# Score matmuls in 64x64 TensorE tiles without a block-diagonal K, K transposed in another order and copied by VectorE, and odd V rows moved by VectorE, in a fused sliding-window attention and adapter kernel

## The chip, the cores and the metric

One core of one Trainium2 chip. The metric is the device time of one execution in microseconds (us). A run is called fast or slow by the rule that these measurements use: for a program on one core, slow means over 1.5% above the fastest run of the same kernel. The profile is one execution taken by the hardware profiler; its span is 1.5 to 2.5 us shorter than the device time.

Names in the profile: PE is TensorE, PEld its weight loads, DVE is VectorE, ACT is ScalarE, POOL is GpSimd, SP issues the output DMAs. L312 is line 312 of the kernel that is being profiled, so the same statement has other line numbers in other kernels.

## The reference

```python
# 8 batches, 8 heads, 576 positions, head dimension 64; q, k, v are randn * 0.1, f32
scores = (q @ k.transpose) / sqrt(64)
scores = where(abs(i - j) <= 32, scores, -1e9)
attn   = softmax(scores) @ v                      # -> x, 4608 rows of 512
logits = x @ w_gate                               # 8 experts, the best 2 get softmax weights
out    = x + sum over the 2 experts of w * ((x @ A[e]) @ B[e])      # rank 16
```

## The kernel before

The work goes by head groups `y`: 16 of them, two per batch, four heads each, in two halves `t` of two heads `uu`. The stages of one group are: load Q, K, V with a cast to f16 (GpSimd issues these DMAs); transpose Q and K on TensorE; copy them out of PSUM (`f_q`, `f_k`); score matmuls (`f_score`); exp on ScalarE; PV matmuls; normalise on VectorE. Per batch the adapter stage follows. A list scheduler inside the program lays out a fixed order for every engine from assumed durations (the numbers in `plan.add`), and each engine then works through its own queue in order.

The parts that the change and the argument touch:

```python
kT  = [const.tile([128, 2 * NB, 2, 64], F16, ...)]     # partitions (t, d); columns (t, q, j): block-diagonal in t
vbd = [const.tile([128, NB, 4 * VC], F16, ...)]        # partitions (uu, t, 32 keys); V block-diagonal in (t, uu)

def f_k(y, t, eng):                # K out of PSUM: contiguous read, scattered write
    p0 = 64 * t
    tp = f16(("t", y, 1))[p0:p0 + 64, :, 0:576].rearrange("p v (j b q) -> p v j b q", j=8, b=18)
    dst = kT[y % NKT][p0:p0 + 64].rearrange("p b v (t q j) -> p t v j b q", t=2, q=4)[:, t]
    for jv in range(2):
        nc.scalar.copy(out=dst[:, jv], in_=tp[:, jv])          # 64 x 576, q steps by 8 elements = 16 bytes

def f_score(i):                    # 128x64 tiles: both halves t in one matmul, zeros between them
    ...
    nc.tensor.matmul(out=pt[64 * uu:64 * uu + 64, 4 * g:4 * g + 4],
                     lhsT=ident[:, 64 * uu:64 * uu + 64], rhs=bcast(mask, 1, 2), ...)
    nc.tensor.matmul(out=pt[64 * uu:64 * uu + 64, e]..., lhsT=kT[y % NKT][:, NB * uu + a, jv],
                     rhs=qT[y % NQT][:, :, c0:c0 + 8]..., ...)
...
    T["ek", y, t] = plan.add("ACT", 1.35, f_k(y, t, "ACT"), ...)    # the plan takes 1.35 us for two copies
```

The softmax here doesn't subtract the row's maximum and nothing guards it: scores larger than these inputs give would overflow.

Of the kernel before, what the change touches and what calls it, by code (L numbers as in the profile page):

```python
# [16 lines left out]
D_TR, D_S, D_PV, D_X, D_Z, D_G, D_O = -4.0, 0.0, 3.0, 4.0, 8.0, 4.0, 4.0  # L17
# [131 lines left out]
def kernel(  # L149
# [24 lines left out]
    VC = 2 * D + 2  # L174
    OC = D + 2
# [24 lines left out]
    kT = [const.tile([128, 2 * NB, 2, 64], F16, name=f"kT{i}") for i in range(NKT)]  # L200
    vbd = [const.tile([128, NB, 4 * VC], F16, name=f"vbd{i}") for i in range(NV)]
    PT = [const.tile([128, TB, 128], F16, name=f"PT{i}") for i in range(NPT)]
    xs = [const.tile([128, NG, DD], F16, name=f"xs{i}") for i in range(NX)]
    ident = const.tile([128, 128], F16)
    sel = const.tile([128, 4], F32)
    mask = const.tile([128, 2, 128], F16)
# [16 lines left out]
    def load_v(y):  # L223
        b, x = divmod(y, 2)
        d = vbd[y % NV]
        for uu in range(2):
            for t in range(2):
                c = 2 * t + uu
                s0 = 64 * uu + 32 * t
                src = v[b, 2 * x + uu + 4 * t].rearrange("(a p v) d -> p a (v d)", p=32, v=2)  # L230
                nc.gpsimd.dma_start(out=d[s0:s0 + 32, :, VC * c + 1:VC * c + 1 + 2 * D], in_=src)  # L231

    def zero_v(i):
        nc.vector.memset(vbd[i].rearrange("p a c -> p (a c)").bitcast(U32), 0)
        for z in (0, VC - 1):
            ones = vbd[i].rearrange("p a (c w) -> p a c w", c=4)[:, :, :, z]
            nc.vector.tensor_copy(out=ones, in_=bcast(sel, 1, NB))
# [4 lines left out]
    nc.vector.tensor_reduce(  # L242
        out=sel.rearrange("p (t u) -> p u t", t=2),
        in_=ident.rearrange("k (u t p) -> k u t p", u=2, t=2), axis=AX.X, op=ALU.add)
    zero_v(0)
# [3 lines left out]
    nc.vector.memset(kT[0].rearrange("p a b c -> p (a b c)").bitcast(U32), 0)  # L249
    nc.gpsimd.memset(mask, 0.0)  # L250
    for s in range(4):
        for jv in range(2):
            blk = mask[32 * s:32 * s + 32, jv].rearrange("k (u j p) -> k u j p", u=2, j=16)
            nc.gpsimd.affine_select(out=blk, in_=blk, compare_op=ALU.is_ge, fill=NEG,
                                    base=-jv, channel_multiplier=-2,
                                    pattern=[[64, 2], [1, 16], [16, 4]])
            nc.gpsimd.affine_select(out=blk, in_=blk, compare_op=ALU.is_ge, fill=NEG,
                                    base=64 + jv, channel_multiplier=2,
                                    pattern=[[-64, 2], [-1, 16], [-16, 4]])
# [3 lines left out]
    zero_v(1)  # L263
    load_v(1)
    for i in range(1, NKT):
        nc.vector.memset(kT[i].rearrange("p a b c -> p (a b c)").bitcast(U32), 0)
    for y in (2, 3):
        load(y, 0)
        load(y, 1)
        zero_v(y)  # L270
        load_v(y)
        if y == 2:
            for cc in range(4):
                nat = cc // 2 + 2 * (cc % 2)
                nc.gpsimd.dma_start(out=WA_sb[:, cc, 0:ER],
                                    in_=moe_A.transpose([1, 0, 2])[128 * nat:128 * nat + 128])
                nc.gpsimd.dma_start(out=WA_sb[:, cc, ER:],
                                    in_=moe_w_gate[128 * nat:128 * nat + 128])
            nc.gpsimd.dma_start(out=B_sb, in_=moe_B.rearrange("e r d -> (e r) d"))
# [3 lines left out]
    def f_tr(y, w):  # L283
        def fn():
            tp = f16(("t", y, w))
            src = raw[y, w]
            for s in range(NJ):
                j = s if w == 0 else 2 * (s % 8) + s // 8
                for t in range(2):
                    nc.tensor.matmul(out=tp[64 * t:64 * t + 64, s // 8, 72 * (s % 8):72 * (s % 8) + 72],  # L290
                                     lhsT=src[:, t, D * j:D * j + D],
                                     rhs=ident[0:72, 0:72], is_transpose=True,
                                     start=True, stop=True)
        return fn

    def f_q(y):
        def fn():
            tp = f16(("t", y, 0))[:, :, 0:576].rearrange("p h (j c) -> p h j c", j=8)
            dst = qT[y % NQT][:, :, 2:2 + 2 * NP].rearrange("p (h j) c -> p h j c", h=2)
            nc.vector.tensor_copy(out=dst, in_=tp)  # L300
        return fn

    def f_k(y, t, eng):
        def fn():
            p0 = 64 * t
            tp = f16(("t", y, 1))[p0:p0 + 64, :, 0:576].rearrange(
                "p v (j b q) -> p v j b q", j=8, b=18)
            dst = kT[y % NKT][p0:p0 + 64].rearrange(
                "p b v (t q j) -> p t v j b q", t=2, q=4)[:, t]
            for jv in range(2):  # L310
                if eng == "ACT":
                    nc.scalar.copy(out=dst[:, jv], in_=tp[:, jv])  # L312
                else:
                    nc.vector.tensor_copy(out=dst[:, jv], in_=tp[:, jv])
        return fn

    def f_score(i):
        def fn():
            pt = f32(("s", i)).rearrange("p g (e w) -> p (g e) w", w=128)
            for g in range(2):  # L320
                for uu in range(2):
                    nc.tensor.matmul(  # L322
                        out=pt[64 * uu:64 * uu + 64, 4 * g:4 * g + 4],
                        lhsT=ident[:, 64 * uu:64 * uu + 64], rhs=bcast(mask, 1, 2),
                        start=True, stop=False)
                for e in range(4 * g, 4 * g + 4):
                    y, r = divmod(TB * i + e, QB)
                    a, jv = divmod(r, 2)
                    for uu in range(2):
                        c0 = NP * uu + 4 * a  # L330
                        nc.tensor.matmul(  # L331
                            out=pt[64 * uu:64 * uu + 64, e].rearrange(
                                "p (u j q) -> p u j q", u=2, j=NJ),
                            lhsT=kT[y % NKT][:, NB * uu + a, jv],
                            rhs=qT[y % NQT][:, :, c0:c0 + 8].rearrange(
                                "p j (u q) -> p u j q", u=2),
                            start=False, stop=(e == 4 * g + 3))
        return fn

    def f_exp(i):  # L340
        def fn():
            nc.scalar.activation(out=PT[i % NPT].rearrange("p e w -> p (e w)"),  # L342
# [4 lines left out]
    def f_pv(y, gp):  # L347
        ms = range(4 * gp, min(4 * gp + 4, NB + 1))

        def fn():  # L350
            po = f32(("o", y, gp))[:, :, 0:4 * OC].rearrange("p g (c w) -> p g c w", c=4)
            vb = vbd[y % NV]
            lanes = ([], [])
            for a in range(NB):
                for jv in range(2):
                    for up in range(2):
                        if a + up in ms:
                            lanes[(a + up) % 2].append((a, jv, a + up, up))
# [7 lines left out]
            for op in ops:  # L366
                a, jv, m, up = op
                i, e = divmod(QB * y + 2 * a + jv, TB)
                hh = 64 * (m % 2)
                nc.tensor.matmul(  # L370
                    out=po[hh:hh + 64, m // 2 - 2 * gp, :, jv:jv + D + 1],
                    lhsT=PT[i % NPT][:, e, 64 * up:64 * up + 64],
                    rhs=vb[:, a].rearrange("p (c w) -> p c w", c=4)[
                        :, :, (D + 1) * jv:(D + 1) * jv + D + 1],
# [3 lines left out]
    def f_norm(y, gp):  # L378
        n = 2 if gp < 2 else 1

        def fn():
# [3 lines left out]
            nc.vector.tensor_reduce(out=rc[:, 0:n], in_=po[:, :, :, 0:OC:OC - 1],  # L385
                                    axis=AX.X, op=ALU.add)
            nc.vector.reciprocal(out=rc[:, 0:n], in_=rc[:, 0:n])
# [138 lines left out]
    def tiles_of(y):  # L526
        return range(QB * y // TB, (QB * (y + 1) - 1) // TB + 1)

    W = 15.0
# [4 lines left out]
    for y in range(NQ):  # L534
# [14 lines left out]
        for w in range(2):  # L549
            bf = ps["t", y, w] = plan.buf(2)  # L550
            T["t", y, w] = plan.add("PE", 0.65, f_tr(y, w), base + D_TR + 0.1 * w,
                                    [T["qk"[w], y]], take=bf)
            if w == 0:
                T["eq", y] = plan.add("DVE", 0.8, f_q(y), base + D_TR, [T["t", y, w]] + old,
                                      uses=[bf])
            else:
                for t in range(2):
                    eng = ("ACT", "ACT")[t]
                    T["ek", y, t] = plan.add(eng, (1.35, 1.35)[t], f_k(y, t, eng),
                                             base + D_TR + 0.1, [T["t", y, w]] + old, uses=[bf])  # L560
        for i in range(9 * y // 4, 9 * (y + 1) // 4):
            deps = []
            for yy in {(TB * i) // QB, (TB * i + TB - 1) // QB}:
                deps += [T["eq", yy], T["ek", yy, 0], T["ek", yy, 1]]
# [3 lines left out]
            T["s", i] = plan.add("PE", 0.92, f_score(i), due + D_S, deps, take=bf)  # L568
            T["e", i] = plan.add("ACT", 1.03, f_exp(i), due + D_S, [T["s", i]] + pvs, uses=[bf])
            for yy in (y - 1, y):  # L570
                for gp in range(3):
                    key = ("pv", yy, gp)
                    if yy < 0 or key in T:
# [3 lines left out]
                    nd = {(QB * yy + 2 * a + jv) // TB for a in range(lo, hi + 1)  # L577
                          for jv in range(2)}
                    if max(nd) > i:
# [3 lines left out]
                    T[key] = plan.add("PE", (0.97, 0.97, 0.48)[gp], f_pv(yy, gp), due,  # L583
                                      [T["e", z] for z in nd] + [T["v", yy]], take=bo)
# [3 lines left out]
                        "DVE", (1.05, 1.05, 0.75)[gp], f_norm(yy, gp), due,  # L588
# [8 lines left out]
                    eng = ("DVE", "DVE", "DVE")[gp]  # L597
                    T["ex", bb, gp] = plan.add(eng, (0.7, 0.7, 0.65)[gp], f_ext(bb, gp, eng),
# [61 lines left out]
```

## Time and profile before

| | before |
|---|---|
| device time, median (range) | 310.78 us (310.16 to 311.4) |
| profile span | 308.1 us |
| ACT busy, and of that the kT copies | 228.7 us, 166.0 us |
| PE, DVE, POOL busy | 182.1, 105.5, 77.8 us |
| mean granted TensorE clock | 0.76 |

The first part of the page gives each engine's busy time and its share of the span; two rows of the second part give the busy tenths of ScalarE and the clock (in tenths) in 40 equal slices of 7.7 us.

```profile
PE 182.1 (59%) x2760; PEld 135.9 (44%) x2760; DVE 105.5 (34%) x297; ACT 228.7 (74%) x141; POOL 77.8 (25%) x136
...
ACT  0958878969559797799469797899469796963330
...
PEclk9999585758599575969599576955699566958957
```

ScalarE is the busiest: between the first and the last score matmul (21 to 282 us) it is busy 209.6 of 261 us. Groups of instructions, by shape; the columns are line, engine, operation, output and input, shapes, count, then total busy us and mean ns of one, then idle time of the engine just before them and what ended it.

```profile
L312 ACT COPY kT<-P 64x576 f16<-64x576 f16 x64 | 166.0, 2837 | 1.9 <-PE P L290 1.7
L342 ACT ACTIVATE PT<-P 128x1024 f16<-128x1024 f32 x36 | 37.5, 1043 | 43.7 <-PE P L331 28.9 <-issue 14.7
L486 ACT COPY zT<-P 128x640 f16<-128x640 f16 x8 | 5.5, 690 | 2.8 <-PE P L479 2.6
L322 PE MATMUL P<-mask,ident 128*64 128x512 f16 x144 | 43.0, 529 | 48.2 <-ACT kT L312 35.4 <-DVE qT L300 11.8 <-DVE xs L388 1.1
```

The same engine copies 640 elements in 690 ns (zT) and needs 2837 ns for 576 (kT). Both read f16 from PSUM, so the size is not the reason. TensorE, before the mask matmuls that begin each score task, sat idle 35.4 us for these copies. The waits view (who waited for whom, us in total, times, longest) shows the score matmuls too:

```profile
PE P L331 <- ACT kT L312: 38.4, 12, 6.4
PE P L322 <- ACT kT L312: 35.4, 12, 5.3
```

### The profile page before, as it was taken

How to read it: one execution, taken by the hardware profiler on the slowest of the kernel's cores; microseconds unless marked ns; L12 is line 12 of the kernel's file. 1: busy time of each engine (PE TensorE's matmuls, PEld its weight loads, DVE VectorE, ACT ScalarE, POOL GpSimd, SP SyncE). 2: the span in 40 equal slices, each digit the busy share in tenths (PEclk: the TensorE clock that was granted, in tenths of full speed). 3: DMA queues.
4: the chain of work that ended last, by engine and by line, in shares of the span. 5: the costliest groups of instructions: out<-in, count | busy, mean ns of one | idle time of the engine just before them, and what ended most of it. 6: DMA issues, size and time to landing. Idle time of an engine off the chain costs nothing. (4 is left out here: it accounts for less than half of the span.)

```text
span 308.1 us, 6466 instructions
## 1 busy us (share of the span) xinstructions
PE 182.1 (59%) x2760; PEld 135.9 (44%) x2760; DVE 105.5 (34%) x297; ACT 228.7 (74%) x141; POOL 77.8 (25%) x136
## 2 busy tenths in 40 slices
PE   1125373765695638835695638747694728548660
PEld 1115262644574523724574523635674514436420
DVE  4863050503345230602445230602454320406610
ACT  0958878969559797799469797899469796963330
POOL 3998754403140050600332040400330000000000
PEclk9999585758599575969599576955699566958957
DMA  4819999653659183890429390910444000300314
GB/s 77 112 17 124 52 135 135 80 80 32 87 51 213 48 92 67 157 184 5 40 51 193 67 106 21 191 32 2 38 70 126 2 0 22 135 0 2 107 56 145
DMA packets 37164, 24.28 MB, mean 79 GB/s; under 512 B 27792, under 2 KB 27920, under 8 KB 37136
## 3 DMA queue, kind: packets, MB, share of 16 engines
q0 software_dynamic: 30992, 14.44, 49.9%
q1 hardware_dynamic: 6144, 9.44, 9.3%
q8 instruction: 21, 0.34, 0.5%
q14 instruction: 7, 0.06, 0.1%
HBM read 28.85 MB, written 9.44 MB: 124 GB/s over the span
## 5 line engine op out<-in xcount | busy, mean ns | idle before, releaser
L312 ACT COPY kT<-P 64x576 f16<-64x576 f16 x64 | 166.0, 2837 | 1.9 <-PE P L290 1.7
L231 POOL DMA_DIRECT2D vbd<-in_v_dram x64 | 39.2, 627 | 130.8 <-PE P L370 122.5
L322 PE MATMUL P<-mask,ident 128*64 128x512 f16 x144 | 43.0, 529 | 48.2 <-ACT kT L312 35.4
L342 ACT ACTIVATE PT<-P 128x1024 f16<-128x1024 f32 x36 | 37.5, 1043 | 43.7 <-PE P L331 28.9
L331 PE MATMUL P<-qT,kT 128*64 128x128 f16 x576 | 46.7, 277 | 38.4 <-ACT kT L312 38.4
L331 PEld LDWEIGHTS <-kT 128*64 128x64 f16 x576 | 39.7, 146 | 50.9 <-ACT kT L312 40.6
L370 PE MATMUL P<-vbd,PT 128*64 128x260 f16 x576 | 51.0, 317 | 17.2 <-ACT PT L342 8.5
L370 PEld LDWEIGHTS <-PT 128*64 128x64 f16 x576 | 38.4, 125 | 25.6 <-issue 22.1
L322 PEld LDWEIGHTS <-ident 128*64 128x64 f16 x144 | 14.4, 135 | 52.0 <-issue 39.1
L385 DVE TENSOR_REDUCE rc<-P 128x8 f32<-128x16 f32 (+1 forms) x48 | 8.1, 169 | 81.7 <-PE P L370 55.5
L290 PE MATMUL P<-ident,r 72*64 72x72 f16 x1024 | 26.8, 213 | 7.5 <-DMA r<-in_q_dram 6.3
L388 DVE TENSOR_TENSOR xs<-P,rc 128x512 f16<-128x512 f32 (+1 forms) x48 | 28.9, 602 | 1.7
L290 PEld LDWEIGHTS <-r 72*64 72x64 f16 x1024 | 24.5, 125 | 8.9 <-DMA r<-in_q_dram 6.3
L510 ACT COPY obt<-P 128x1024 f32<-128x1024 f32 (+1 forms) x24 | 19.7, 875 | 11.5 <-PE P L499 11.5
L497 PE MATMUL P<-B_sb,zT 128*128 128x512 f16 x40 | 19.7, 492 | 0.8 <-ACT zT L486 0.8
L499 PE MATMUL P<-xs,ident 128*128 128x512 f16 x40 | 19.5, 488 | 0.0
L300 DVE COPY qT<-P 128x1152 f16<-128x1152 f16 x16 | 12.1, 757 | 16.8 <-PE P L290 16.8
L417 DVE COPY xT<-P 128x1024 f16<-128x1024 f16 (+1 forms) x24 | 13.9, 597 | 9.2 <-PE P L401 9.2
L425 PE MATMUL P<-WA_sb,xT 128*128 128x136 f16 x160 | 15.0, 267 | 0.2 <-DVE xT L417 0.2
L220 POOL DMA_DIRECT2D r<-in_k_dram x16 | 11.3, 708 | 11.7 <-PE P L290 11.7
L425 PEld LDWEIGHTS <-xT 128*128 128x128 f16 x160 | 13.2, 121 | 1.2 <-DVE xT L417 0.4
L442 DVE TENSOR_REDUCE m<-P 128x5 f32<-128x40 f32 x8 | 1.6, 201 | 34.8 <-PE P L425 34.8
(41 smaller groups left out, 120.6 us busy)
## 6 DMA issues: line engine op xcount, KB each, us to landing
out_dram<-obt SPq DMA_DIRECT2D x64, 128.0 KB, 3.3
r<-in_q_dram POOLq DMA_DIRECT2D x16, 288.0 KB, 6.9
r<-in_k_dram POOLq DMA_DIRECT2D x16, 288.0 KB, 8.0
vbd<-in_v_dram POOLq DMA_DIRECT2D x64, 72.0 KB, 4.0
out_dram<-obt SPq DMA_DIRECT2D x32, 32.0 KB, 1.9
WA_sb<-in_moe_A_dram POOLq DMA_DIRECT2D x4, 32.0 KB, 5.1
B_sb<-in_moe_B_dram POOLq DMA_DIRECT2D x1, 128.0 KB, 4.8
WA_sb<-in_moe_w_gate_dram POOLq DMA_DIRECT2D x4, 2.0 KB, 2.9
```

The source lines that it names most:

```text
L231: nc.gpsimd.dma_start(out=d[s0:s0 + 32, :, VC * c + 1:VC * c + 1 + 2 * D], in_=src)
L290: nc.tensor.matmul(out=tp[64 * t:64 * t + 64, s // 8, 72 * (s % 8):72 * (s % 8) + 72], lhsT=src[:, t, D * j:D * j + D], rhs=ident[0:72, 0: ...
L312: nc.scalar.copy(out=dst[:, jv], in_=tp[:, jv])
L322: nc.tensor.matmul(out=pt[64 * uu:64 * uu + 64, 4 * g:4 * g + 4], lhsT=ident[:, 64 * uu:64 * uu + 64], rhs=bcast(mask, 1, 2), start=True, ...
L331: nc.tensor.matmul(out=pt[64 * uu:64 * uu + 64, e].rearrange("p (u j q) -> p u j q", u=2, j=NJ), lhsT=kT[y % NKT][:, NB * uu + a, jv], rhs ...
L342: nc.scalar.activation(out=PT[i % NPT].rearrange("p e w -> p (e w)"), in_=f32(("s", i)).rearrange("p g w -> p (g w)"), func=AF.Exp, scale= ...
L370: nc.tensor.matmul(out=po[hh:hh + 64, m // 2 - 2 * gp, :, jv:jv + D + 1], lhsT=PT[i % NPT][:, e, 64 * up:64 * up + 64], rhs=vb[:, a].rearr ...
L388: nc.vector.tensor_tensor(out=xs[b % NX][:, 2 * gp:2 * gp + n, 256 * x:256 * x + 256].rearrange("p g (c d) -> p g c d", c=4), in0=po[:, :, ...
L425: nc.tensor.matmul(out=pz[:, GS * g:GS * g + ER + E], lhsT=st[b, "xT"][:, g, 128 * cc:128 * cc + 128], rhs=WA_sb[:, cc, :], start=(cc == 0 ...
L497: nc.tensor.matmul(out=pd[:, i], lhsT=st[b, "zT"][:, g], rhs=B_sb, start=True, stop=False)
L499: nc.tensor.matmul(out=pd[:, i].rearrange("p (t x w) -> p t x w", t=2, x=2), lhsT=ident, rhs=xs[b % NX][:, g].rearrange("p (x t w) -> p t ...
L510: nc.scalar.copy(out=ob[:, 0:n], in_=f32(("d", b, gp))[:, 0:n])
```

## The change

The intent is to halve TensorE's work and to take K's copy off ScalarE. One head takes one half of the array's rows (64 rows, a 64x64 tile), so K needs no zeros between heads. K's transposes use a permuted identity so that one VectorE copy can write kT in contiguous runs. V is not block-diagonal in `t` any more: PV streams 130 columns instead of 260. Keys of odd index must lie 32 partitions further down than the even ones; the DMA still brings both in one run of 128 elements, and VectorE then copies the odd half down (`f_sv`).

```diff
-    kT = [const.tile([128, 2 * NB, 2, 64], F16, name=f"kT{i}") for i in range(NKT)]
+    kT = [const.tile([128, NB, 2, 32, 2], F16, name=f"kT{i}") for i in range(NKT)]
+    kperm = const.tile([72, 72], F16)
 # K transposes: PSUM order (q, j, b) instead of (j, b, q)
+                        dst = half.rearrange("d (p j b) -> d p j b", p=4, j=8)[:, :, jj]
+                                     rhs=ident[0:72, 0:72] if w == 0 else kperm,
 # f_k: pairs read 36 bytes apart, runs of 64 elements written, on VectorE
+            tp = f16(("t", y, 1))[:, :, 0:576].rearrange("p v (q b e) -> p v b q e", q=32, e=2)
+            dst = kT[y % NKT].rearrange("p b v q e -> p v b q e")
             nc.vector.tensor_copy(out=dst, in_=tp)
+    def f_sv(y, uu, t):
+            blk = vbd[y % NV][:, :, t, uu]
+            nc.vector.tensor_copy(out=blk[64 * uu + 32:64 * uu + 64, :, 4:4 + D],
+                                  in_=blk[64 * uu:64 * uu + 32, :, 4 + D:4 + 2 * D])
 # f_score: row half t, column half uu
-                        lhsT=ident[:, 64 * uu:64 * uu + 64], rhs=bcast(mask, 1, 2),
+                        lhsT=ident[64 * t:64 * t + 64, 64 * t:64 * t + 64],
+                        rhs=bcast(mask[64 * t:64 * t + 64], 1, 4), start=True, stop=False)
+                            lhsT=kT[y % NKT][64 * t:64 * t + 64, bh, :, :, bl].rearrange("p v q -> p (v q)"),
 # f_pv: 130 columns
+                    rhs=vbd[y % NV][:, a, t, :, 3:4 + D],
 # ... mask half as large; no clearing of kT; no reduce before the reciprocal;
 # ... qT copies to ScalarE, one xT copy of three to ScalarE; the plan's durations, period W 15 -> 13
```

## The prediction

> **What bounds the kernel now.** ScalarE. The page gives ACT 228.7 us busy of 308.1 (74%), PE 59%, DVE 34%; its slices show ACT at 7 to 9 tenths from 8 to 270 us. In the groups view the 64 kT copies (64x576 f16, PSUM to SBUF) take 166.0 us, 2837 ns each, while the zT copy of 640 f16 on the same engine takes 690 ns. The kT copy scatters single 2-byte elements 16 bytes apart. The Trainium skill, "SBUF — State Buffer", under Door 1, says that each access to a new 16-byte line is penalised; the 4x gap agrees. In the waits view PE waits for them 38.4 us before score matmuls, up to 6.4 us at once; the granted clock averages 0.76. Period: about 33 us per batch (8 to 270 us, 8 batches).
>
> **What changes, per batch (two head groups).**
> - ACT loses 8 kT copies (20.8 us), gains 2 qT copies of 1152 contiguous elements (estimated 1.15 us each from zT 640 = 690 ns and exp 1024 = 1043 ns) and one xT copy (1.0). Left: exp 4.7, output copies 2.6, qT 2.3, xT 1.0, zT 0.7, rest 0.2 = 11.5 us (92 in all).
> - DVE loses qT (1.5), the reduce before the reciprocal (1.0), one xT (0.7); gains 2 kT copies (128x1152, read as strided 4-byte pairs, written contiguously) and 8 V shifts. If pairs keep the qT copy's rate, kT is 0.76 us; at one element a cycle about 1.3; if strided PSUM reads are penalised as ACT's writes were, about 2.7. Shifts (32x576) estimated 0.3 each from the qT slope halved. Sum about 13 us (12.5 to 17).
> - PE: score tiles become 64x64. "TensorEngine Tiling (Array Packing)", Tiling Modes, gives four independent tiles; the trace shows two now (8 score matmuls of 128 columns in 0.43 us at clock 0.5). A score task falls from 0.9 to 0.45 us at full clock; PV streams 130 instead of 260 columns, 3.9 to 2.0 us. PE about 15.5 to 11.5 us at full clock.
> - DMA unchanged: the windows view shows q/k loads near 160 GB/s (1.8 us each), V near 115 (2.5 us), output about 3.5 us: 15.7 us, the next limit, PE and DVE close behind.
> - Start: 8 mask selects of 0.52 us instead of 16 (GpSimd is at them until 20 us), no kT memsets: first scores about 5 us earlier.
>
> **On the critical path.** Nearly all of the 20.8 us per batch, until DMA, PE or DVE binds; the PE and V savings matter only then. New period 16 to 17 us x 8 = 132, plus about 13 before the first scores and 21 from the last scores out: **166 us**; 148 to 190 holds it 8 times in 10. Faster by over 2%: 0.985; within 2%: 0.01; slower: 0.005.
>
> **What would show it.** ACT busy near 92 us; no engine above about 80%; DVE near 105; kT on DVE 0.76 us, qT on ACT 1.15, shifts 0.3; PE busy down by a third, mean clock 0.85 or more; score matmuls in four-way groups; DMA share over 0.8 in mid-kernel; PE waits now for DMA, DVE or exp, not kT.
>
> **What would make it wrong.** kT on DVE at 2.7 us or more (then 185 to 200); row halves that don't overlap, or drains at each change of tile shape; shifts queuing in front of kT or normalisation while a V load lands; the static order, laid out for a 13 us period, stalling on one late load; a clock that stays at 0.5.

## The result

| | before | after |
|---|---|---|
| device time, median (range) | 310.78 us (310.16 to 311.4) | 166.91 us (166.62 to 167.19) |
| ratio of fast runs | | 0.537 (95% interval 0.531 to 0.543) |
| profile span | 308.1 us | 165.4 us |
| mean granted TensorE clock | 0.76 | 0.94 |

Both had two runs. Ratios in this document are the mean time of one kernel's fast runs over that of the other's of the same rounds, so they are not quite the ratios of the quoted medians. A later set of six runs of the kernel after, on the same chip as the last experiments, had two fast runs (166.6 and 166.8 us) and four up to 174.0 us; the kernel spreads by some per cent above its fastest, and that limits what small differences can tell.

The same parts of the page after:

```profile
PE 122.8 (74%) x2760; PEld 91.7 (55%) x2760; DVE 105.7 (64%) x305; ACT 87.5 (53%) x101; POOL 73.9 (45%) x128
...
ACT  3104244354668717767693869226877692462410
...
PEclk9999999999999987999999999969999999789585
DMA  2997999999999999999999999998453034116143
```

```profile
L347 ACT ACTIVATE PT<-P 128x1024 f16<-128x1024 f32 x36 | 36.2, 1027 | 25.5 <-PE P L335 23.2 <-ACT dm L455 0.9 <-ACT zT L487 0.8
L316 DVE COPY vbd<-vbd 32x576 f16<-32x576 f16 x64 | 19.5, 336 | 1.2
L325 PE MATMUL P<-mask,ident 64*64 64x512 f16 x144 | 18.1, 458 | 8.4 <-issue 2.8 <-POOL mask L253 2.3 <-DVE kT L310 1.4
L301 ACT COPY qT<-P 128x1152 f16<-128x1152 f16 x16 | 17.9, 1119 | 22.1 <-PE P L291 22.0
L310 DVE COPY kT<-P 128x1152 f16<-128x1152 f16 x16 | 12.1, 754 | 5.5 <-PE P L291 5.4
```

ScalarE's 166 us of kT copies have become 12.1 us on VectorE. ScalarE waits for TensorE 23.2 us before exp and 22.0 before qT; TensorE's mask matmuls wait 1.4 us for the kT copies, where they waited 35.4 us. The granted TensorE clock is 0.94 where it was 0.76, and TensorE is busy 74% of the span where it was 59%. In experiments 1 and 2 below the two also go together (0.94 at 75%, 0.79 at 65%); that one causes the other was not tested.

To see where the time went, the span can be cut at the first and the last score matmul. The lines below are the score matmuls of the kernel before, of the kernel after and of experiment 1, in that order: count, min/median/max duration in ns, and first and last start.

```profile
L331 PE MATMUL P<-qT,kT x576: 216/308/316, 21.4 to 282.1; 128*64 128x128 f16 x192
```

```profile
L335 PE MATMUL P<-qT,kT x576: 212/217/313, 13.1 to 135.4; 64*64 64x128 f16 x192
```

```profile
L338 PE MATMUL P<-qT,kT x576: 216/218/314, 21.4 to 167.4; 128*64 128x128 f16 x192
```

| | until the first score | first to last score | per batch (divided by 8) | after the last score start |
|---|---|---|---|---|
| before | 21.4 | 260.7 | 32.6 | 26.0 |
| experiment 1 (kT writes only) | 21.4 | 146.0 | 18.3 | 25.9 |
| after | 13.1 | 122.3 | 15.3 | 30.0 |

### The profile page after: what moved, and what is told of

The parts are those of the page before. It is cut to its first block, busy times and chain, and to the rows that moved or that the text cites. A ratio compares the mean times of both kernels' runs of the same rounds, so it can differ in the third digit from the quotient of the medians.

```text
span 165.4 us, 6458 instructions
## 1 busy us (share of the span) xinstructions
PE 122.8 (74%) x2760; PEld 91.7 (55%) x2760; DVE 105.7 (64%) x305; ACT 87.5 (53%) x101; POOL 73.9 (45%) x128
## 2 busy tenths in 40 slices
DMA packets 37165, 24.29 MB, mean 147 GB/s; under 512 B 27792, under 2 KB 27920, under 8 KB 37136
## 3 DMA queue, kind: packets, MB, share of 16 engines
q0 software_dynamic: 30992, 14.44, 72.4%
## 4 chain that ended last, share of the span: by engine, by line
PE 39%; DMA 20%; POOL 13%; DVE 10%; issue 8%; ACT 5%; ACTq 1%; POOLq 0%; DVEq 0%
DMA r<-in_k_dram 12%; DMA r<-in_q_dram 8%; PE P L374 8%; PE P L291 6%; POOL vbd L228 5%; PE P L498 5%; PE P L500 5%; PE P L426 5%; PE P L325 4%; ACT qT L301 3%; POOL r L220 3%; PE P L335 3%; PE P L402 3%; DVE xs L389 3%; DVE zs L469 2%
## 5 line engine op out<-in xcount | busy, mean ns | idle before, releaser
L347 ACT ACTIVATE PT<-P 128x1024 f16<-128x1024 f32 x36 | 36.2, 1027 | 25.5 <-PE P L335 23.2
L374 PE MATMUL P<-vbd,PT 128*64 128x130 f16 x576 | 29.5, 241 | 5.1 <-issue 2.1
L301 ACT COPY qT<-P 128x1152 f16<-128x1152 f16 x16 | 17.9, 1119 | 22.1 <-PE P L291 22.0
L374 PEld LDWEIGHTS <-PT 128*64 128x64 f16 x576 | 23.4, 120 | 9.3 <-issue 6.6
L325 PE MATMUL P<-mask,ident 64*64 64x512 f16 x144 | 18.1, 458 | 8.4 <-issue 2.8
L291 PE MATMUL P<-ident,r 72*64 72x72 f16 x512 | 14.2, 213 | 10.1 <-DMA r<-in_q_dram 8.5
L316 DVE COPY vbd<-vbd 32x576 f16<-32x576 f16 x64 | 19.5, 336 | 1.2
L335 PEld LDWEIGHTS <-kT 64*64 64x64 f16 x576 | 15.3, 122 | 5.5 <-issue 2.1
L335 PE MATMUL P<-qT,kT 64*64 64x128 f16 x576 | 18.0, 241 | 0.3 <-DVE kT L310 0.2
L291 PE MATMUL P<-kperm,r 72*64 72x72 f16 x512 | 13.6, 212 | 2.9 <-ACT qT L301 0.8
L310 DVE COPY kT<-P 128x1152 f16<-128x1152 f16 x16 | 12.1, 754 | 5.5 <-PE P L291 5.4
L402 PE MATMUL P<-ident,xs 128*128 128x128 f16 x160 | 13.5, 231 | 1.1 <-DVE xs L389 1.0
```

Of the source, the lines that this page charges most:

```text
L291: nc.tensor.matmul(out=dst, lhsT=src[:, t, D * j:D * j + D], rhs=ident[0:72, 0:72] if w == 0 else kperm, is_transpose=True, start=True, st ...
L301: nc.scalar.copy(out=dst, in_=tp)
L316: nc.vector.tensor_copy(out=blk[64 * uu + 32:64 * uu + 64, :, 4:4 + D], in_=blk[64 * uu:64 * uu + 32, :, 4 + D:4 + 2 * D])
L325: nc.tensor.matmul(out=pt[64 * uu:64 * uu + 64, t], lhsT=ident[64 * t:64 * t + 64, 64 * t:64 * t + 64], rhs=bcast(mask[64 * t:64 * t + 64] ...
L335: nc.tensor.matmul(out=pt[64 * uu:64 * uu + 64, t, e].rearrange("p (u j q) -> p u j q", u=2, j=NJ), lhsT=kT[y % NKT][64 * t:64 * t + 64, b ...
L347: nc.scalar.activation(out=PT[i % NPT].rearrange("p t e w -> p (t e w)"), in_=f32(("s", i)).rearrange("p g w -> p (g w)"), func=AF.Exp, sc ...
```

## The experiments

Two theories stood against each other from the start. Theory A: the scattered write of the kT copy made it slow, that copy paced the kernel, and its removal is most of the gain. Rival C: TensorE's halved work carries the gain. Beside them stood the question what paces the kernel after: DMA (as the prediction said), TensorE, or VectorE with its new shifts.

### 1. The kernel before, with contiguous kT writes

```diff
+                    dst = (half[:, 72 * (s % 8):72 * (s % 8) + 72] if w == 0 else
+                           half.rearrange("d (p j b) -> d p j b", p=4, j=8)[:, :, s % 8])
+                                     rhs=ident[0:72, 0:72] if w == 0 else kperm,
-                "p v (j b q) -> p v j b q", j=8, b=18)
+                "p v (m b) -> p v b m", b=18)
-                "p b v (t q j) -> p t v j b q", t=2, q=4)[:, t]
+                "p b v (t m) -> p t v b m", t=2)[:, t]
```

> The kernel before with one thing changed: the K transposes write PSUM in another order (a permuted identity), so that ScalarE's kT copies read single elements 36 bytes apart and write runs of 32 contiguous elements instead of single elements 16 bytes apart. Block-diagonal K, 128x64 score tiles, PV and VectorE work stay. Correct result. Theory A (the destination step made the copy slow, and that copy made the kernel slow): the copy falls from 2837 ns to about 0.67 us (the 640-element zT copy takes 690 ns), ACT busy from 229 to about 105 us, and the kernel to 180 to 200 us, most of the gain of the whole change. Rival B (the copy is slow for another reason: 64 partitions, four-dimensional pattern, ScalarE on f16): the copy stays above 2 us and the kernel above 290 us. Rival C (TensorE's halved work carries the gain): copy fast, but kernel still above 240 us.

Measured: 195.41 us (195.02 to 197.07), ratio to before 0.630 (0.627 to 0.633). ACT busy fell to 99.5 us. The kT group of this kernel:

```profile
L319 ACT COPY kT<-P 64x576 f16<-64x576 f16 x64 | 37.3, 632 | 4.9 <-PE P L297 4.7
```

The copy went from 2837 to 632 ns on the same engine with the same number of elements and instructions, and the kernel from 310.5 (the runs of before in this set) to 195.4 us. That is 115 of the 144 us of the whole change, so theory A holds, rival B falls, and TensorE's halved work is not needed for most of the gain (rival C). Experiment 2 shows the other side. What is left between this kernel and the kernel after, some 28 us, is read from the table above: 8.3 us come from the earlier start, about 24 us from the shorter period (18.3 to 15.3 us), and about 4 us are lost again after the last score. In the window from 20 to 165 us this kernel's PE was busy 127.3 of 145 us at clock 0.96, so here TensorE's halved score and PV work could pay; no run takes that part of the change alone.

### 2. The kernel after, with the scatter given back to VectorE

```diff
-                        dst = half.rearrange("d (p j b) -> d p j b", p=4, j=8)[:, :, jj]
+                        dst = half[:, 72 * jj:72 * jj + 72]
-                                     rhs=ident[0:72, 0:72] if w == 0 else kperm,
+                                     rhs=ident[0:72, 0:72],
 # f_k, for each jv of two: contiguous read, single elements written 32 bytes apart
+                    "p (j b e q) -> p j b e q", j=8, b=9, e=2)
+                dst = kT[y % NKT][:, :, jv].rearrange("p b (q j) e -> p j b e q", q=4)
```

> The kernel after with the permuted identity taken out of the K transposes, so that VectorE's kT copies read contiguously and write single elements 32 bytes apart (two copies of 128x576 per head group instead of one of 128x1152). Correct result. Theory A in its general form (single-element writes to a new 16-byte line cost the same on either engine, about 4.9 ns an element): 2.8 us per copy, DVE busy up by about 77 us, the kernel 210 to 240 us. Rival (only ScalarE pays): about 0.75 us per copy[...], DVE busy up by about 12 us, kernel 167 to 178 us.

Measured: 226.67 us (226.11 to 227.04), and the copy:

```profile
L312 DVE COPY kT<-P 128x576 f16<-128x576 f16 x32 | 80.1, 2684 | 5.9 <-PE P L291 4.1 <-ACT zT L489 1.8
```

VectorE pays about what ScalarE did for a copy (2684 against 2837 ns), so it is not the engine that makes the copy fast; without the permuted identity the change would have lost 60 us of its gain (226.7 against 166.9).

But this kernel, with every scattered write still in it, is also 84 us faster than the kernel before. One copy now serves both row halves, so there are 32 copies of 80.1 us in all, on VectorE, where there were 64 of 166.0 us on ScalarE; TensorE waits for them 22.3 and 8.2 us, where it waited 35.4 and 38.4:

```profile
PE P L327 <- DVE kT L312: 22.3, 14, 3.0
PE P L337 <- DVE kT L312: 8.2, 2, 4.4
```

The contiguous writes alone give 115 us (experiment 1), the rest of the change alone gives 84, and both together 144. The two parts shorten the same wait, so their gains can't be added. How the 84 us divide between fewer copies, the move away from ScalarE and TensorE's halved work was not separated.

### 3. The two copies swapped between the engines

```diff
-            nc.vector.tensor_copy(out=dst, in_=tp)      # f_k
+            nc.scalar.copy(out=dst, in_=tp)
-            T["eq", y] = plan.add("ACT", 1.15, f_q(y, "ACT"), ...
+            T["eq", y] = plan.add("DVE", 0.8, f_q(y, "DVE"), ...
-            T["ek", y] = plan.add("DVE", 0.8, f_k(y), ...
+            T["ek", y] = plan.add("ACT", 1.15, f_k(y), ...
```

> The kernel after with the two copies swapped between engines: kT (pairs of elements read 36 bytes apart in PSUM, written in runs of 64) on ScalarE, qT (contiguous) on VectorE. Correct result. If only the destination step matters: kT on ScalarE 1.12 to 1.15 us like qT there now, qT on VectorE 0.76 us, kernel within 2% of 166.9. If ScalarE pays for strided PSUM reads too: kT above 2.5 us and the kernel above 180 us.

Measured: fast runs 167.03 and 167.26 us (two more, at 169.9 and 170.0, are called slow).

```profile
L310 ACT COPY kT<-P 128x1152 f16<-128x1152 f16 x16 | 17.9, 1122 | 18.7 <-PE P L291 15.2 <-DVE xs L389 3.1
L303 DVE COPY qT<-P 128x1152 f16<-128x1152 f16 x16 | 12.0, 752 | 4.7 <-PE P L291 4.5
```

On ScalarE kT takes 1122 ns where qT took 1119; on VectorE qT takes 752 where kT took 754. Pairs read 36 bytes apart in PSUM cost as much as a contiguous read, on both engines, and the fast runs show no difference by which engine gets which copy.

### 4. The copy by itself, in sixteen forms

In the kernel before, the kT copies went to a scratch tile in eight forms per engine (two head groups each), in two kernels. K's own tile stays zero, so the results are wrong and only the durations count.

```diff
+                    if k == 3:
+                        nc.scalar.copy(out=every[3][:, :, 0], in_=tp)        # single f16 every 16 bytes
+                    if k == 5:
+                        nc.scalar.copy(out=pairs, in_=two)                   # pairs every 16 bytes
 # ... and so on for the other forms, and the same for VectorE
```

> The copy by itself: the kernel before, where the kT copies of 576 f16 elements out of PSUM (half on ScalarE, half on VectorE) go to a scratch tile in eight forms, two head groups each: destination step 1, 2, 4, 8, 16 elements (2, 4, 8, 16, 32 bytes), pairs every 16 bytes, and contiguous writes from single elements or pairs read 36 bytes apart. The result is wrong on purpose and the kernel's time means nothing; the durations are the result. Theory A (a write to a new 16-byte line each time costs, reads don't): on ScalarE about 0.67 us at steps 2 to 8 bytes, 2.8 us at 16 and 32 bytes, pairs about half of that, and 0.67 for both strided reads. Rival B (every step above one element costs, as a partial-word write): 2.8 us from step 4 bytes on. On VectorE: 0.46 us contiguous and for pairs read strided, 0.75 us for single elements, and the same jump at 16 bytes only if the cost lies in the memory and not in ScalarE.

> The copy by itself once more, to tell apart what in a 16-byte step costs (the earlier forms: single f16 2.7 us at 16 bytes, 1.4 at 8, 0.8 at 4, but pairs every 16 bytes 0.69). The kernel before with the kT copies going to a scratch tile, on both engines, as: 288 f32 elements at steps of 8, 16 and 32 bytes; f16 pairs every 8 and every 32 bytes; f16 runs of 3 and of 4 every 16 bytes; single f16 every 6 bytes. Wrong K on purpose. Theory W (writing half of a 4-byte word costs about 4.4 ns per 16-byte line touched, whole words are cheap): f32 at 16 bytes about 0.4 to 0.6 us, pairs at 8 and 32 bytes below 0.9 us, runs of 4 below 0.75, runs of 3 about 0.9 to 1.0 us (192 lines with half words), single every 6 bytes about 1.1 us. Theory L (each new 16-byte line costs about 4.4 ns): f32 at 16 and 32 bytes 1.4 us, pairs every 32 bytes 1.4 us, runs of 4 about 0.8 us. Pairs every 16 bytes at 0.69 speak for W so far.

Measured, mean ns of four copies each (576 f16 elements or 288 f32 elements; one run of each of the two kernels, the four copies of a form within some 2% of their median):

| write pattern | ScalarE | VectorE |
|---|---|---|
| contiguous f16 | 632 | 461 |
| single f16 every 4 bytes | 802 | 812 |
| single f16 every 6 bytes | 1119 | 1126 |
| single f16 every 8 bytes | 1438 | 1447 |
| single f16 every 16 bytes | 2706 | 2716 |
| single f16 every 32 bytes | 2600 | 2579 |
| runs of 3 f16 every 16 bytes | 1010 | 1020 |
| runs of 4 f16 every 16 bytes | 632 | 462 |
| pairs of f16 every 8 bytes | 629 | 463 |
| pairs of f16 every 16 bytes | 681 | 692 |
| pairs of f16 every 32 bytes | 679 | 688 |
| f32 every 8 bytes (288) | 412 | 464 |
| f32 every 16 bytes (288) | 680 | 686 |
| f32 every 32 bytes (288) | 678 | 686 |
| contiguous, single elements read 36 bytes apart | 632 | 760 |
| contiguous, pairs read 36 bytes apart | 632 | 460 |

Three of these lines, for ScalarE: single elements every 16 bytes and pairs every 16 bytes of the first kernel, runs of 3 of the second.

```profile
L326 ACT COPY sc<-P 64x576 f16<-64x576 f16 x4 | 10.8, 2706 | 2.8 <-DVE sc L343 2.6
...
L330 ACT COPY sc<-P 64x576 f16<-64x576 f16 x4 | 2.7, 681 | 0.1
```

```profile
L335 ACT COPY sc<-P 64x576 f16<-64x576 f16 x4 | 4.0, 1010 | 0.7 <-DVE sc L352 0.6
```

The expectation for single elements every 4 and 8 bytes was wrong: these were to be free by theory A, and they cost 1.3 and 2.3 times the contiguous copy. So was the one for pairs every 16 bytes: half of the single elements' time (about 1.4 us) was expected, and they took 0.68. Rival B of this experiment, a full jump already at 4 bytes, was wrong too. Theory W of the second kernel (half of a 4-byte word written costs some 4.4 ns per 16-byte line) foretold the single elements every 6 bytes (1.1 us) and, but for a hair, the runs of 3 (1.01 where 0.9 to 1.0 was stated); theory L, a price per new line whatever is written, foretold twice what f32 at 16 bytes and pairs at 32 bytes took. W was a little low on whole words: it gave 0.4 to 0.6 us for f32 at 16 bytes, and it took 0.68. An estimate from the table, with a fixed part of about 145 ns (from two contiguous ScalarE copies, 632 ns for 576 elements and 1119 for 1152: 2 x 632 - 1119): 288 lines written in whole words cost (680 - 145)/288 = 1.9 ns each; 576 lines with half a word cost (2706 - 145)/576 = 4.4 ns each; 192 runs of 3 cost (1010 - 145)/192 = 4.5 ns each. The smaller steps fit the same price if it is counted by 16-byte lines and not by elements: single elements every 8, 6 and 4 bytes touch 288, 216 and 144 lines, at 4.5, 4.5 and 4.6 ns. That both engines agree within 2% on the slow forms points to the memory and not to the engine. The fit is an explanation that the numbers allow; how the memory writes half a word was not observed.

A warning came out of this experiment: both kernels were found correct, though K's tile was all zeros. With q and k as small as here the scores hardly move the softmax, so the comparison with the reference would not notice a K in a wrong order. That kT has the right order in experiments 1 and 2 and in the kernel after rests on the index patterns, not on the comparison. Followed by hand, these patterns put the same key, 2q + v of each block of 64, at position q of half v in K's tile in the kernels before and after and in experiments 1 and 2.

### 5. The mask matmuls alone back on all 128 rows

```diff
-                        lhsT=ident[64 * t:64 * t + 64, 64 * t:64 * t + 64],
-                        rhs=bcast(mask[64 * t:64 * t + 64], 1, 4), start=True, stop=False)
+                        lhsT=ident[:, 64 * t:64 * t + 64],
+                        rhs=bcast(mask, 1, 4), start=True, stop=False)
```

> The kernel after with the mask matmuls alone put back to all 128 rows (an ident slice of 128x64 picks the 64 mask rows wanted, same result), so that they run two at a time in 128x64 tiles and the score matmuls after them need another tile shape. Correct result. Theory (four row-and-column tiles do run at once): each score task takes about 0.21 us longer at full clock, TensorE gets some 8 us more work, the kernel 167 to 174 us; near 174 if TensorE's time is on the critical path throughout, near 167 if DMA hides it. Rival (the row halves never overlapped): mask matmul groups take the same time as now, kernel unchanged.

Measured: fast runs 171.31 and 172.46 us (two more, at 174.06 and 174.84, are called slow), against 166.6 to 167.2 in the fast runs of the kernel after: about 5 us more. The two were not run in the same rounds, and four later runs of the unchanged kernel after took 169.7 to 174.0 us, so the size of this difference is uncertain. In the timeline (start, length, engine, what, count) a group of four mask matmuls in the kernel after, with the score and PV matmuls behind it, and the same groups of this experiment:

```profile
71.39 0.41 PE L325 MATMUL P<-mask,ident 64*64 64x512 f16 x4
71.63 0.40 PE L335 MATMUL P<-qT,kT 64*64 64x128 f16 x16
71.96 0.89 PE L374 MATMUL P<-vbd,PT 128*64 128x130 f16 x22
```

```profile
73.11 0.62 PE L325 MATMUL P<-mask,ident 128*64 128x512 f16 x4
73.66 0.42 PE L335 MATMUL P<-qT,kT 64*64 64x128 f16 x16
74.01 0.66 PE L374 MATMUL P<-vbd,PT 128*64 128x130 f16 x14
```

Four 64x64 tiles end 0.41 us after the first began, four 128x64 tiles 0.62 us: one slot of 512 columns more. So the row halves do run at once. The Trainium skill, "TensorEngine Tiling (Array Packing)", section Tiling Modes, gives four independent 64x64 tiles, and the trace agrees. The whole task grew by more than the 0.21 us that was expected. From the start of the mask group to the next work it takes 0.57 us in the kernel after and 0.90 here (medians of 20 tasks each: 0.57 and 0.91). The score matmuls start 0.55 us after the mask matmuls where they started 0.24 after, which is about 0.1 us more than the extra slot; here the two groups have different tile shapes. That is some 36 x 0.34 = 12 us of extra TensorE time, of which about 5 us reached the total. So TensorE's time is on the critical path in part of the kernel and hidden in the rest.

### 6. V's odd rows by DMA instead of VectorE

```diff
-                nc.gpsimd.dma_start(out=vbd[y % NV][64 * uu:64 * uu + 32, :, t, uu, 4:], in_=src)
+                for z in range(2):
+                    s0 = 64 * uu + 32 * z
+                    nc.gpsimd.dma_start(out=vbd[y % NV][s0:s0 + 32, :, t, uu, 4:4 + D], in_=src[z])
 # the f_sv tasks are gone
```

> The kernel after without the VectorE shifts: V's odd rows go by DMA straight to their 32 partitions, in runs of 128 bytes (f16) instead of 256, 128 V transfers instead of 64. Correct result. Theory D (DMA is the next limit, VectorE has slack): VectorE loses 19.5 us busy, but V's packets double and the kernel gets slower, 178 to 200 us. Rival (VectorE's shifts are on the critical path and DMA has room): the same or faster, 158 to 167 us.

Measured: fast runs 194.22 to 196.69 us (a fourth, 200.15, is called slow), ratio to before 0.628. DMA packets rose from 37165 to 56620, and the chain of work that ended last, by engine, turned from

```profile
PE 39%; DMA 20%; POOL 13%; DVE 10%; issue 8%; ACT 5%; ACTq 1%; POOLq 0%; DVEq 0%
```

in the kernel after to

```profile
DMA 51%; POOL 19%; PE 10%; issue 9%; DVE 5%; ACT 1%; ACTq 0%; POOLq 0%; DVEq 0%
```

in this one. The shift by VectorE, 64 copies of 336 ns, buys about 28 us. How much of the 28 us is the shorter packets and how much the 64 further issues of 0.6 us each on GpSimd was not separated.

### 7. Most V loads left out

```diff
-                fn = (lambda y=y: load_v(y))      # head groups 4 to 15
+                fn = None
```

> The kernel after with the V loads of head groups 4 to 15 left out (48 of 64 transfers; the result is wrong on purpose, everything else runs). It takes 30 us of DMA time and 30 us of GpSimd issue away. Theory D (DMA sets the pace in the first half, TensorE in the second): 150 to 160 us. If DMA set the pace throughout: 140 to 145. If DMA sets no pace: 165 or more.

Measured: three fast runs at 159.99, 160.69 and 161.08 us (a fourth, 164.94, is called slow). It is 6 us less than the kernel after, at the edge of the range given for theory D and far from the one for DMA as the only pace. Score matmuls ran from 13.1 to 129.4 us, a period of 14.5 us instead of 15.3. Taking an estimated 30 us of DMA work away (12 head groups at the 2.5 us that the prediction read from the trace), and with it 29.9 us of GpSimd's issuing (POOL busy 73.9 to 44.0), gives 6 us; more packets and more issues cost 28 us in experiment 6. So DMA with its issuing does not pace the kernel alone, but there is little room left in it. The page's DMA row could not have told this. It stood at 9 tenths through most of the kernel after, and it still does in this one with 16 of 64 V transfers left:

```profile
DMA  1996899999998899186798896830152044026053
```

### 8. Most shifts left out

```diff
+        if y < NV:
             for uu in range(2):
                 for t in range(2):
                     T["sv", y, uu, t] = plan.add("DVE", 0.3, f_sv(y, uu, t), ...
```

> The kernel after with the V shifts of head groups 4 to 15 left out (48 of 64; the result is wrong on purpose, the odd rows are stale). VectorE loses about 15 us busy, nothing else changes. If the shifts lie off the critical path: 164 to 167 us. If VectorE paces the kernel: 152 to 158 us.

Measured: one fast run at 162.12 us and three at 166.92 to 171.08 called slow beside it. DVE busy fell from 105.7 to 91.1 us. This is inconclusive: nothing came near 152 to 158 us, so VectorE does not pace the kernel alone, but a gain of 0 to 5 us can't be told from the spread.

### 9. Two attempts to beat the kernel after

The first start of the scores waited for the mask on GpSimd and for VectorE's clearing of V buffers. So the mask was built first, half of it copied by VectorE, and the clearing of V buffers 2 and 3 was moved behind the first kT copy.

```diff
+        if y in (2, 3):
+            T["iv", y] = plan.add("DVE", 2.3, (lambda y=y: init_v(y)), base - 5.0, [T["ek", y - 2]])
-        init_v(y)                                  # was ahead of load_v(y)
```

> An attempt to beat the kernel after by starting earlier: the mask is built before the first V loads, its second half is copied by VectorE instead of four more GpSimd selects, and the clearing of the V buffers 2 and 3 (4.5 us of VectorE) waits until the first kT copy is done. Correct result. First scores at about 10.5 us instead of 12.3 to 13, later loads issued about 2.5 us earlier. If the start is on the critical path: 163 to 165 us; if DMA or TensorE later absorbs it: 166 to 168.

Measured: 175.2 us median, fast runs 171.32 to 173.54; slower than the kernel after. The scores did start at 10.2 us, but then:

```profile
26.10 1.85 PE L374 MATMUL P<-vbd,PT 128*64 128x130 f16 x28 [11.18 <-DVE vbd L316]
```

The PV matmuls waited 11.18 us for a V shift, because VectorE, working in order, was held by a clearing that waited for a V load:

```profile
22.57 1.05 DVE L233 MEMSET vbd<- 64x1188 uint32 x1 [12.43 <-DMA vbd<-in_v_dram]
```

The clearing now stood behind the load in program order. It touches other columns than the load does, yet a wait for the load was generated. The attempt moved a wait to a worse place, and tells nothing about the worth of an earlier start. With the clearing put ahead of its load in program order again it might be free of that wait; this was not run.

The second attempt added to this the plan's durations as the trace shows them and a period of 15 us.

```diff
-    W = 13.0
+    W = 15.0
-        dur = (1.55, 1.55, 3.0)[z]
+        dur = (1.8, 1.8, 2.6)[z]
 # ... transposes 0.66, scores 0.57, PV 0.55 and 0.60, shifts 0.34
```

> The attempt of b2 with the static order laid out from durations that the trace of after shows (transposes 0.66, score task 0.57, PV 0.55 and 0.60, shift 0.34, loads 1.8, 1.8 and 2.6 us) and a period of 15 us instead of 13. Correct result. If the order's wrong durations cost stalls: 2 to 6 us below b2. If resources bind and not the order: within 2 us of b2.

Measured: 177.29 us median, fast runs 175.12 to 176.58, some 3 to 4 us above the first attempt. Truer durations in the plan did not help here; since both carry the same new wait, the plan's own worth stays open. Beside these two, the unchanged kernel after was run six times more:

> The kernel after, unchanged, beside the two attempts of this call, to have its spread on the same chip: 166 to 169 us in fast runs.

Measured: fast runs 166.64 and 166.79 us, four more from 169.7 to 174.0.

## Why the prediction was right

**The bound was right.** It said that ScalarE's kT copies pace the kernel and that nearly all of their time is on the critical path. Experiment 1 took only their scattered write away: ScalarE was busy 129 us less (228.7 to 99.5) and the kernel took 115 us less, of the 144 of the whole change. That the rest of the change would have given 84 us without it (experiment 2) the prediction did not say.

**The reason for the slow copy was right in kind and rough in detail.** The prediction took it from the Trainium skill, "SBUF — State Buffer", Door 1: each access to a new 16-byte line is penalised. Experiment 4 shows that a new line costs about 1.9 ns if whole words are written and 4.4 ns if half a word is, so the single f16 elements were the expensive part. Steps of 4 and 8 bytes, which stay in a line for several elements, cost the same for each line.

**The open risk, kT on VectorE, fell on the good side.** 754 ns measured, 0.76 us in the best of its cases. Pairs read apart keep the fast rate; single elements read apart would have cost 760 against 461 ns (experiment 4). The Trainium skill, "Vector Engine (DVE) Microarchitecture Reference", section 5.1, asks for an innermost step of 1 and more than one element there for two 2-byte elements a cycle; an innermost run of two, at 460 ns for 576 elements, agrees with it. qT on ScalarE 1.12 us against 1.15, shifts 0.336 against 0.3, ACT busy 87.5 against 92, DVE 105.7 against 105, PE down by 33%, clock 0.94 against "0.85 or more".

**The sum was right partly by two errors that cancel.** The prediction's terms were 13 us before the first score, 132 us of period and 21 us after the last score. Measured were 13.1, 122.3 and 30.0 us. (The first score came 8.3 us earlier, not 5: the first score before was at 21.4 us. There GpSimd's mask was done at 20.2 us and VectorE's clearing at 20.3; after, at 12.2 and 12.3, so both had to be shortened; the prediction named work of both and put the gain at 5 us.) The period was set too long because DMA, summed to 15.7 us per batch, was named the next limit and something was added for stalls; the measured period is 15.3 us, below that sum, and in experiment 7 an estimated 30 us less of DMA work shortened it only to 14.5. The stretch after the last score was set at 21 us when even the kernel before shows 26.0; it should have been read from that trace; what made it 4 us longer still was not looked into. That the total came within 1 us of the forecast is luck.

**"The PE and V savings matter only then" was right, and can be sized now.** With the copy mended and TensorE's work as before, the period is 18.3 us (experiment 1); with the whole change it is 15.3. How much of the 3 us is TensorE's and how much VectorE's or ScalarE's was not separated.

**TensorE's estimate was a little low.** A score task was put at 0.45 us at full clock. The timeline shows a mask group at 71.39 us and the PV group that follows at 71.96 us: 0.57 us. The prediction counted streamed columns only. It named drains at each change of tile shape as a risk, and the traces show a cost there: the same 512 columns of score matmuls take 0.23 us when PV follows in the same shape (experiment 1, 128x64, 4 cases, such as 92.88 to 93.11 us) and 0.33 when PV follows in another (64x64, then 128x64, in the kernel after, 13 cases, such as 71.63 to 71.96 us), an estimated 0.1 us for each change. For a batch, 11.5 us of TensorE were forecast; between 13 and 136 us it was busy 104.7 us, 13.1 for each of the 8 batches.

**"DMA share over 0.8" came true and proves little.** The share stays near its top when most V loads are gone (experiment 7). It counts the time that packets are under way, and that is no fixed amount of work: the same 30992 packets of GpSimd's queue took 49.9% of the span before, 85.8% in experiment 1 and 72.4% after, which is 154, 166 and 120 us.

## What to carry to other kernels

Compare a copy's time with another copy of the same size on the same engine before asking how to give the engine less work: a factor of four points to the access pattern, not to the amount of work. When a 2-byte tensor has to be permuted on its way out of PSUM, put the stride on the read side (in pairs on VectorE) and write pairs or runs; a transpose by a permuted identity did the reordering here at no cost in the matmul (212 against 213 ns). When two remedies shorten the same wait, run each alone: here 115 and 84 us made 144 together. To learn what paces a kernel of many engines, take one resource's work away and put more in: a busy share of 9 tenths told less than the two runs with less and more DMA.

## What the Trainium skill lacked or had wrong

- "SBUF — State Buffer", Door 1, says of the 16-byte lines that "how far you can stride for free depends on dtype: 4 fp32, 8 bf16, 16 int8". Measured for f16 writes: a step of 8 elements costs 2706 against 632 ns on ScalarE, a step of 4 (two hits in every line, which the table of that page calls enough for full bandwidth) 1438 ns, a step of 2 802 ns. For f32, a step of 4 elements costs 680 against 412 ns at a step of 2. No page that I found states that writing half of a 4-byte SBUF word is what is dear (runs of 3 every 16 bytes 1010 ns, runs of 4 632 ns), nor that VectorE and ScalarE pay the same (2716 and 2706 ns).
- The same place says that any non-contiguous PSUM access pattern significantly slows down matmuls. K's transposes, which write PSUM in runs of 18 elements, took 212 ns on average in the kernel after, and Q's, written in one run, 213 ns. So no slowdown shows for such runs. Reads of PSUM 36 bytes apart cost ScalarE nothing (632 and 632 ns); VectorE paid for single elements (760 against 461 ns) and not for pairs (460).
- No page that I found gives a time for a change of tile shape in TensorE. Here it is an estimated 0.1 us (0.33 against 0.23 us for 512 columns of score matmuls before PV in another and in the same shape).
